# First batch's keys and values taken out of PSUM by two masked factors over all partitions, with three pieces of work re-ordered and the verdict's product later

## The chip, the cores and the metric

One core of one Trainium2 chip runs the whole kernel. The metric is the device time of one execution in microseconds; the runs' median counts.

## The reference

An attention with a memory of 32 slots (`M`) in 8 batches of 8 heads, followed by a layer of 8 experts with top-1 gating. Cut to what matters:

```python
# q, k, v: (8, 8, 576, 64); phi: (8, 8, 576, 32)
a = np.exp(phi - np.max(phi, axis=2, keepdims=True))
a = a / (np.sum(a, axis=2, keepdims=True) + 1e-09)
k_m = np.einsum('bhsm,bhsd->bhmd', a, k)          # keys of the memory
v_m = np.einsum('bhsm,bhsd->bhmd', a, v)          # values of the memory
scores = (1 / np.sqrt(64)) * np.matmul(q, k_m.transpose(0, 1, 3, 2))
attn = softmax(scores)                            # with 1e-09 in the sum
x = np.matmul(attn, v_m)                          # -> (4608, 512)
logits = x @ w_gate + modality_bias[modality_id]
e_idx = np.argmax(logits, axis=1); gate_w = softmax(logits)[e_idx]
out[mask_e] = gate_w * (np.maximum(x @ w1[e], 0) @ w2[e])   # mask_e: tokens of expert e
```

## The kernel before, in words

The kernel guesses one expert for all tokens from the first token's bias (`guess`), loads that expert's weights, and computes with them. At the end a verdict tells whether every token did choose that expert (`others`, `verdict`: DVE reduces `badp` to `bad`, PE adds it over the partitions by one product with `ones_c`, DVE writes `bad_i`, and every engine reads `bad_i` and branches). For other inputs a general path follows, which isn't entered here.

The 8 heads lie as 4 heads (`HG`) in each of 2 groups (`NG`); a group's 4 heads times 32 slots fill the 128 partitions. For a later batch the products of the memory (`kv_products`) are made head by head, each into its own 32 partitions and 64 columns. For the first batch, `first_products(t)` (t = 0 keys, t = 1 values) takes two heads at once: the weights of heads j and j+1 against both heads' 64 columns, so that 64 partitions x 128 columns are written, of which two blocks of 32 x 64 are wanted: head j even in columns 0 to 63, head j odd in columns 64 to 127. The other two blocks are products of one head's weights with the other head's keys. `first_sums` makes the sums of the weights into column 128.

`first_divide` adds EPS to the sums, takes the reciprocal `rec`, and `first_blocks(0, g)` copies the wanted blocks, times `rec`, into `keys`, head by head: 4 ACT instructions for group 0 and 4 DVE instructions for group 1. `first_blocks(1, g)` does the same for `values`, with 8 ACT instructions. `keys` are written twice side by side (the `o` axis of length 2).

What follows in the first batch: `first_keys` transposes the keys on PE and ACT copies them out (`kT`); `scores` multiplies them with the queries, which DVE has turned in place before (`q_turn`, in halves of heads); `soften` (DVE: turn, maximum, difference; ACT: exponential, one for each group in this part of the batch); `first_values` turns the values (`vT`); `value_products` multiplies vT with the first weights w1 (`raw`), giving `vwh` and `vwl` (an upper and a lower part of fp32); `normalise`, `a_split` (`xah`, `xal`); then `hidden` (x with vw, 128 or 320 columns wide) and `outputs` (with w2), which fill nearly all of the PE's time. `warm(n)` issues n products of zeros, fillers, into a bank that nobody reads.

The order of instructions is one program order for all engines, found when the kernel is built: `plan_first` and its like list stages by `add(name, kind, after, what, ...)`, and `weave` merges the attention's list with the experts' list by a model of durations (`TAKES`), floors (`floor`) and due times (`due`, in progress of the experts' products). Each engine runs its own instructions in that order, and waits by semaphores. Transfers are issued from SP's queue (and two small ones from ACT's).

Of the kernel before, what the change touches and what calls it, by code (L numbers as in the profile page):

```python
# [8 lines left out]
F32 = mybir.dt.float32  # L9
# [3 lines left out]
AF = mybir.ActivationFunctionType  # L13
# [41 lines left out]
def attn_moe(ctx: ExitStack, tc: tile.TileContext, q, k, v, phi, mod_id, w_gate, mod_bias, w1, w2, out):  # L55
# [22 lines left out]
    EPS = 1e-9  # L78
    BUSY = 92, 10

# [19 lines left out]
    ident = const.tile([P, P], F32, name="ident")  # L100
    ones_c = const.tile([P, 1], F32, name="ones_c")
    busy = const.tile([P, 512], BF16, name="busy")
    wg = const.tile([P, KCH, E], F32, name="wg")
# [235 lines left out]
    def first_products(t):  # L339

        pe = by_rows(live["pe", 0][0])
        pk = None if t else pair_of_banks(1)
        to = two_banks() if t else [pk[:, g] for g in range(NG)]
        live["first", t] = to

        tiles = [(j, g, slice(QP * g, QP * (g + 1))) for j in range(0, HG, 2) for g in range(NG)]
        for c in range(QC):
            for j, g, half in tiles:
                nc.tensor.matmul(  # L349
                    to[g][M * j:M * (j + 2), 0:2 * D].rearrange("p (j d) -> p j d", j=2),  # L350
                    lhsT=pe[half, c, j:j + 2].rearrange("p j m -> p (j m)"), rhs=kv_sb[half, t, j:j + 2, c * D:(c + 1) * D],
                    start=(c == 0), stop=(c == QC - 1), tile_position=(QP * g, M * j),
                )
# [11 lines left out]

    def first_divide():
        den = wk.tile([P, NG], F32, name="den")
        for g in range(NG):
            nc.vector.tensor_scalar_add(den[:, g:g + 1], live["first", 0][g][:, 2 * D:2 * D + 1], EPS)
        rec = wk.tile([P, NG, 1], F32, name="rec")  # L370
        nc.vector.reciprocal(rec[:, :, 0], den)
        live["rec"] = rec
        live["keys", 0] = wk.tile([P, 2, NG, 2, BL], F32, name="keys", bufs=2)
        live["values", 0] = wk.tile([P, NG, D], F32, name="values", bufs=2)
        for g in range(NG):
            first_blocks(0, g)

    def first_blocks(t, g):

        for j in range(HG):  # L380
            rows = slice(M * j, M * (j + 1))
            src = live["first", t][g][rows, D * (j % 2):D * (j % 2 + 1)]
            rec = live["rec"][rows, g]
            if t:
                nc.scalar.activation(live["values", 0][rows, g], src, AF.Copy, scale=rec)  # L385
                continue
            src = src.rearrange("p (u o d) -> p u o d", u=2, o=1).broadcast_to([M, 2, 2, BL])
            if g:
                nc.vector.tensor_scalar(live["keys", 0][rows, :, g], src, rec, None, op0=ALU.mult)
            else:  # L390
                nc.scalar.activation(live["keys", 0][rows, :, g], src, AF.Copy, scale=rec)

# [330 lines left out]
    def first_w2(c):  # L723
# [13 lines left out]
        "vwp": (1.15, ""), "vwu": (0.0, "A1.15"), "vwl": (0.0, "D1.35"),  # L737
# [42 lines left out]
    def plan_first():  # L780
# [4 lines left out]
        def nothing(n, name="pa"):  # L785
            add(("nothing", len(attention)), "nothing", [], warm, n, False, name)
# [13 lines left out]
        add(("exp", 0), "first exp", [("top", 0)], mem_exp, 0)  # L800
        nothing(4)
        add(("prepare",), "nothing", [], prepare)
        turns(0, 0, 11.0)
        add(("sums", 0), "first sums", [("exp", 0)], mem_sums, 0)
        add(("k", 0), "k0", [("exp", 0)], first_products, 0, floor=10.8)
        add(("ks", 0), "nothing", [("sums", 0)], first_sums)
        add(("kn", 0), "kn0", [("k", 0), ("sums", 0)], first_divide)
        turns(0, 1, 11.0)
        nothing(2)
        add(("kT", 0), "kT", [("kn", 0)], first_keys)  # L810
        add(("s", 0, 0), "s0", [("kT", 0), ("qt", 0, 0, 1)], scores, 0, 0, RA)
        add(("e", 0, 0, 0), "e", [("s", 0, 0)], soften, 0, 0, None, 0)
        add(("v", 0), "v0", [("exp", 0)], first_products, 1, floor=15.2)
        add(("vn", 0, 0), "vn0", [("v", 0)], first_blocks, 1, 0)
        add(("vn", 0, 1), "vn0", [("v", 0)], first_blocks, 1, 1)
        add(("e", 0, 0, 1), "e", [], soften, 0, 0, None, 1)
        add(("more", 0), "nothing", [], more_keys, 0)
        add(("kvT", 0), "vT", [("vn", 0, 1)], first_values)
        turns(1, 0, 16.8)
# [14 lines left out]
    def plan_steps(b, dues):  # L834
# [49 lines left out]
        if b == B - 1:  # L884
            stage(attention, ("v",), "verdict", [("others", pair)], verdict, due=due + 6.0)

# [125 lines left out]
    with tc.manual_schedule():  # L1012
# [148 lines left out]
```

## Time and profile before

| what | value |
|---|---|
| median of 3 runs | 407.84 us (406.47 to 408.52) |
| profiled execution | 408.26 us, its span 406.5 us |
| PE busy | 386.9 us, 95% of the span |
| DVE, ACT, POOL busy | 239.1, 146.5, 40.1 us |
| first hidden product | starts at 32.69 us |
| the verdict's product | starts at 360.79 us |

The span runs from the first instruction to the last of the profiled execution; its time has some 1.8 us around that. "PE" are the products, "PEld" the loads of their stationary operand, "SPq" SP's issue of transfers. In rows of instructions the columns are start, duration, engine, line, operation, out<-in, shapes, count, and in brackets the idle time of the engine before and who ended it. In rows of stretches the columns are the stretch, its length, the busy time and count of PE, PEld, DVE, ACT and POOL, the granted PE clock (1.00 is full), the DMA engines' busy share and GB/s. In rows of groups: busy us in total, mean ns of one, idle time before. In rows of waits: us in total, times, the longest. In rows of transfers: count, KB each, us from issue to landing.

### The profile page before, as it was taken

Reading aid. Unit: us, or ns where it says so; the run is one execution under the profiler, and the core shown is the slowest. Engines: PE = TensorE matmul, PEld = TensorE weight load, DVE = VectorE, ACT = ScalarE, POOL = GpSimd, SP = SyncE. Lnnn points to the kernel's source line nnn. Section 1 sums busy time; section 2 is a strip of 40 time slices with the busy share of each in tenths; the row PEclk is TensorE's granted clock in tenths of the full one; section 3 lists DMA queues with packets and bytes.
Section 4 is the critical chain, followed back from the end, with each engine's and each line's share of the span. In section 5 each row is a group of like instructions: output and inputs, shape, how many; then the busy total and the mean of one; then the engine's idle time right before and its main releaser. Section 6 shows DMA issues by size and latency. Waiting matters only on the chain.

```text
span 406.5 us, 10089 instructions
## 1 busy us (share of the span) xinstructions
PE 386.9 (95%) x4234; PEld 308.3 (76%) x4234; DVE 239.1 (59%) x586; ACT 146.5 (36%) x350; POOL 40.1 (10%) x79
## 2 busy tenths in 40 slices
PE   6579999999999999999999999999999999989994
PEld 2347796788778878787968879688877879678983
DVE  2556774976598546862587457764488437760400
ACT  1338243434433324342442325343342425341410
POOL 3136302002000200002000200002000200000000
PEclk8869999999999999999999999999999999999998
DMA  6998146915471391617611293523501011341112
GB/s 232 358 387 312 66 111 207 347 63 169 148 253 53 72 361 52 236 28 250 211 27 28 84 303 101 190 96 82 205 12 42 26 29 29 129 158 26 28 27 58
DMA packets 28967, 56.91 MB, mean 140 GB/s; under 512 B 3312, under 2 KB 8432, under 8 KB 28912
## 3 DMA queue, kind: packets, MB, share of 16 engines
q1 hardware_dynamic: 28624, 56.16, 41.6%
q8 instruction: 35, 0.57, 0.6%
q14 instruction: 20, 0.16, 0.1%
q10 hardware_dynamic: 288, 0.01, 0.0%
HBM read 37.29 MB, written 18.87 MB: 138 GB/s over the span
## 4 chain that ended last, share of the span: by engine, by line
PE 90%; DMA 3%; DVE 3%; ACT 2%; issue 1%; SPq 0%; ACTq 0%
PE pe L690 50%; PE pe L661 23%; PE pair L326 4%; PE pe L628 4%; PE pair L487 3%; DMA q_sb<-in_q_dram 3%; PE pair L575 1%; PE pe L349 1%; PE pair L141 1%; PE pair L628 1%; DVE hl L673 1%; ACT values L385 1%; PE pair L286 1%; ACT hh L670 0%; PE pair L464 0%
## 5 line engine op out<-in xcount | busy, mean ns | idle before, releaser
L690 PE MATMUL pe<-w2h,hh 128*128 128x512 f32 x288 | 117.7, 409 | 0.4 <-DVE hl L673 0.4
L690 PE MATMUL pe<-w2h,hl 128*128 128x512 f32 x288 | 112.6, 391 | 0.0
L690 PE MATMUL pe<-w2l,hh 128*128 128x512 f32 x288 | 110.4, 391 | 0.0
L673 DVE SCALAR_TENSOR_TENSOR hl<-pe,hh 128x256 fp32r<-128x256 f32 (+2 forms) x160 | 58.8, 393 | 55.0 <-ACT hh L670 54.3
L690 PEld LDWEIGHTS pe<-w2h,hh 128*128 128x128 f32 x288 | 54.0, 188 | 24.0 <-issue 11.5
L670 ACT ACTIVATE hh<-pe 128x256 fp32r<-128x256 f32 (+2 forms) x160 | 53.7, 361 | 38.9 <-PE pe L661 38.5
L690 PEld LDWEIGHTS pe<-w2l,hh 128*128 128x128 f32 x288 | 54.0, 188 | 12.0
L690 PEld LDWEIGHTS pe<-w2h,hl 128*128 128x128 f32 x288 | 54.2, 188 | 9.4
L703 ACT ACTIVATE ob<-pe,gates 128x512 f32<-128x512 f32 x36 | 24.7, 689 | 80.3 <-PE pe L690 39.5
L661 PE MATMUL pe<-xbh,vwh 128*128 128x320 f32 x128 | 39.9, 312 | 0.0
L661 PE MATMUL pe<-xbl,vwh 128*128 128x320 f32 x128 | 39.6, 309 | 0.0
L661 PE MATMUL pe<-xbh,vwl 128*128 128x320 f32 x128 | 39.5, 309 | 0.0
L661 PE MATMUL pe<-xah,vwh 128*128 128x256 f32 x128 | 36.2, 291 | 0.2 <-DVE hl L673 0.2
L661 PE MATMUL pe<-xal,vwh 128*128 128x256 f32 x128 | 35.1, 283 | 0.0
L661 PE MATMUL pe<-xah,vwl 128*128 128x256 f32 x128 | 35.0, 282 | 0.0
L257 POOL TENSOR_TENSOR t2sums<-exp 128x512 f32<-128x512 f32 x7 | 9.0, 1287 | 259.4 <-ACT exp L295 259.4
L514 DVE STREAM_TRANSPOSE a<-pair 128x256 f32<-128x256 f32 (+1 forms) x32 | 13.6, 460 | 24.6 <-PE pair L487 24.6
L661 PEld LDWEIGHTS pe<-xah,vwh 128*128 128x128 f32 x128 | 24.0, 191 | 1.7 <-DVE hl L673 1.0
L661 PEld LDWEIGHTS pe<-xbh,vwh 128*128 128x128 f32 x128 | 24.1, 188 | 0.6 <-issue 0.3
L661 PEld LDWEIGHTS pe<-xbl,vwh 128*128 128x128 f32 x128 | 24.1, 188 | 0.3
L661 PEld LDWEIGHTS pe<-xal,vwh 128*128 128x128 f32 x128 | 24.0, 191 | 0.3
L661 PEld LDWEIGHTS pe<-xbh,vwl 128*128 128x128 f32 x128 | 24.1, 188 | 0.0
(132 smaller groups left out, 441.1 us busy)
## 6 DMA issues: line engine op xcount, KB each, us to landing
kv_sb<-in_k_dram SPq DMA_DIRECT2D x8, 1152.0 KB, 5.9
kv_sb<-in_v_dram SPq DMA_DIRECT2D x8, 1152.0 KB, 9.6
out_dram<-ob SPq DMA_DIRECT2D x64, 128.0 KB, 2.4
q_sb<-in_q_dram SPq DMA_DIRECT2D x7, 1152.0 KB, 6.9
ph<-in_phi_dram SPq DMA_DIRECT2D x8, 576.0 KB, 4.1
raw<-in_moe_w_dram SPq DMA_DIRECT2D x2, 1024.0 KB, 8.9
raw<-in_moe_w_dram SPq DMA_DIRECT2D x1, 1280.0 KB, 11.3
out_dram<-ob SPq DMA_DIRECT2D x4, 256.0 KB, 2.0
```

The lines of the kernel that those rows point to most:

```text
L141: nc.tensor.transpose(dst, src, ident[:rows, :rows])
L257: eng.tensor_tensor(t2, src[:, :, 0:4 * M], src[:, :, 4 * M:8 * M], op=op)
L286: nc.tensor.matmul(pb[QP * g:QP * (g + 1), 0:P], lhsT=topc[:, g:g + 1].broadcast_to([P, QP]), rhs=ident, start=True, stop=True, tile_posit ...
L326: nc.tensor.matmul(live["kvp"][M * j:M * (j + 1), g], lhsT=pe[half, j, c * M:(c + 1) * M], rhs=kv_sb[half, :, j, c * D:(c + 1) * D], start ...
L487: nc.tensor.matmul(sc[g][M * j:M * (j + 1), a, c0 * BL:(c0 + n) * BL].rearrange("p (c t) -> p c t", t=BL), lhsT=kTs[b % 2][p0:p0 + BL, u, ...
L514: nc.vector.transpose(a[:, g].rearrange("p a c m -> p a (c m)"), sc[g][:, :, RA * part * BL:(RA * part + n) * BL])
L628: nc.tensor.matmul(pvs[g][M * j:M * (j + 1), :], lhsT=vT[b][rows, j, :], rhs=raw1[rows, j, cols], start=True, stop=True, tile_position=(D ...
L661: nc.tensor.matmul(ph[:, 0:n], lhsT=(vl if k == 2 else vh)[:, g, cols], rhs=xl if k == 1 else xh, start=(g == k == 0), stop=(g == NG - 1 a ...
L670: nc.scalar.activation(hs[0][:, f, h0:h0 + p1 - p0], ph[:, p0:p1], AF.Relu)
L673: nc.vector.scalar_tensor_tensor(hl, ph[:, p0:p1], 0.0, hh.bitcast(F32), op0=ALU.max, op1=ALU.subtract)
L690: nc.tensor.matmul(po, lhsT=tile_columns(hl if n == 1 else hh, f, t), rhs=(w2l if n == 2 else w2h)[:, f, :], start=(f == n == 0), stop=(f ...
L703: nc.scalar.activation(ob, po, AF.Copy, scale=gate_of(b, t))
```

## The change

A constant `places` of 128 x 2 holds, for each partition, 1 in column 0 where its head is even and 1 in column 1 where it is odd, else 0 (8 memsets of 32 x 1 on POOL at the start). `first_divide` multiplies the reciprocals with it: `recs` holds for each group the reciprocal for even heads (0 elsewhere) and for odd heads (0 elsewhere). `first_even(t)` takes columns 0 to 63 of all 128 partitions times the even factor, one ACT instruction for each group; `first_odd(t)` takes columns 64 to 127 times the odd factor and adds the even part, on DVE: four instructions for the keys (a group's two halves of 32 columns, each written twice), two for the values.

Beside it: the sums of the first batch are planned ahead of the first queries' turn; the second group's exponential ahead of the values' blocks; fillers are placed anew (86 small ones at the start instead of 92; 5 instead of 4 ahead of the key products, 4 new behind the sums' products, 2 behind the keys' turn instead of ahead of the division, 2 new ahead of the values' turn); and the verdict is due 12 instead of 6 after the last gate.

```diff
-    BUSY = 92, 10
+    BUSY = 86, 10
+    places = const.tile([P, 2], F32, name="places")
...
     def first_divide():
         den = wk.tile([P, NG], F32, name="den")
-        for g in range(NG):
-            nc.vector.tensor_scalar_add(den[:, g:g + 1], live["first", 0][g][:, 2 * D:2 * D + 1], EPS)
-        rec = wk.tile([P, NG, 1], F32, name="rec")
-        nc.vector.reciprocal(rec[:, :, 0], den)
-        live["rec"] = rec
+        nc.vector.tensor_scalar_add(den, live["sums0"], EPS)
+        rec = wk.tile([P, NG], F32, name="rec")
+        nc.vector.reciprocal(rec, den)
+        recs = wk.tile([P, 2, NG], F32, name="recs")
+        nc.vector.tensor_tensor(
+            recs, rec.rearrange("p (o g) -> p o g", o=1).broadcast_to([P, 2, NG]),
+            places.rearrange("p (e o) -> p e o", o=1).broadcast_to([P, 2, NG]), op=ALU.mult,
+        )
+        live["recs"] = recs
...
-        for g in range(NG):
-            first_blocks(0, g)
-
-    def first_blocks(t, g):
...
+        first_even(0)
+
+    def first_even(t):
+        live["even", t] = wk.tile([P, NG, D], F32, name=f"even{t}")
+        for g in range(NG):
+            nc.scalar.activation(
+                live["even", t][:, g], live["first", t][g][:, 0:D], AF.Copy, scale=live["recs"][:, 0, g:g + 1]
+            )
+
+    def first_odd(t):
+        def add(dst, src, even, g):
+            nc.vector.scalar_tensor_tensor(dst, src, live["recs"][:, 1, g:g + 1], even, op0=ALU.mult, op1=ALU.add)
+        for g in range(NG):
+            src, even = live["first", t][g][:, D:2 * D], live["even", t][:, g]
+            if t:
+                add(live["values", 0][:, g], src, even, g)
+                continue
+            for u in range(2):
+                half = slice(BL * u, BL * (u + 1))
+                add(live["keys", 0][:, u, g], *(
+                    x[:, half].rearrange("p (o d) -> p o d", o=1).broadcast_to([P, 2, BL]) for x in (src, even)
+                ), g)
...
         add(("exp", 0), "first exp", [("top", 0)], mem_exp, 0)
-        nothing(4)
+        nothing(5)
...
-        turns(0, 0, 11.0)
         add(("sums", 0), "first sums", [("exp", 0)], mem_sums, 0)
...
+        nothing(4)
         add(("kn", 0), "kn0", [("k", 0), ("sums", 0)], first_divide)
+        turns(0, 0, 11.0)
+        add(("ko", 0), "ko0", [("kn", 0)], first_odd, 0)
         turns(0, 1, 11.0)
+        add(("kT", 0), "kT", [("ko", 0)], first_keys)
         nothing(2)
-        add(("kT", 0), "kT", [("kn", 0)], first_keys)
...
         add(("v", 0), "v0", [("exp", 0)], first_products, 1, floor=15.2)
-        add(("vn", 0, 0), "vn0", [("v", 0)], first_blocks, 1, 0)
-        add(("vn", 0, 1), "vn0", [("v", 0)], first_blocks, 1, 1)
         add(("e", 0, 0, 1), "e", [], soften, 0, 0, None, 1)
+        add(("vn", 0), "vn0", [("v", 0)], first_even, 1)
+        add(("vo", 0), "ko0", [("vn", 0)], first_odd, 1)
...
-        add(("kvT", 0), "vT", [("vn", 0, 1)], first_values)
+        nothing(2, "pa")
+        add(("kvT", 0), "vT", [("vo", 0)], first_values)
...
-            stage(attention, ("v",), "verdict", [("others", pair)], verdict, due=due + 6.0)
+            stage(attention, ("v",), "verdict", [("others", pair)], verdict, due=due + 12.0)
...
+        for j in range(HG):
+            for e in range(2):
+                nc.gpsimd.memset(places[M * j:M * (j + 1), e:e + 1], float(j % 2 == e))
```

Three places of the resulting order. The first is DVE's queue from the sums (`t2top`, `sums`) to the queries' second turn; `q_sb` is a turn of the queries, `pair` is the PSUM pair with the key products. Before:

```order
L475 STREAM_TRANSPOSE q_sb_99<-q_sb_99 128x2x256
L305 TENSOR_TENSOR t2top<-exp 128x512
L306 TENSOR_TENSOR t2top<-t2top 128x256
L307 TENSOR_TENSOR sums<-t2top 128x128
L308 TENSOR_TENSOR sums<-sums,exp 128x128
L369 TENSOR_SCALAR den<-pair_361 128x1 x2
L371 RECIPROCAL rec<-den 128x2
L389 TENSOR_SCALAR keys<-pair_361,rec 32x2x64 x4
L475 STREAM_TRANSPOSE q_sb_99<-q_sb_99 128x2x256
```

and now, on the same engine at the same place:

```order
L307 TENSOR_TENSOR t2top<-exp 128x512
L308 TENSOR_TENSOR t2top<-t2top 128x256
L309 TENSOR_TENSOR sums<-t2top 128x128
L310 TENSOR_TENSOR sums<-sums,exp 128x128
L373 TENSOR_SCALAR den<-pair_364 128x2
L375 RECIPROCAL rec<-den 128x2
L377 TENSOR_TENSOR recs<-rec,places 128x4
L492 STREAM_TRANSPOSE q_sb_100<-q_sb_100 128x2x256
L397 SCALAR_TENSOR_TENSOR keys<-pair_364,recs,even_418 128x64 x4
L492 STREAM_TRANSPOSE q_sb_100<-q_sb_100 128x2x256
```

The first turn has moved from ahead of the sums to between the division and the key blocks. The second place is ACT's queue from the key blocks to the first weights' copy (`a` is an exponential of `soften`). Before:

```order
L391 ACTIVATE keys<-pair_361,rec 32x2x64 x4
L437 COPY kT_77<-pair_421 128x256
L522 ACTIVATE a<-a 128x256
L385 ACTIVATE values<-pe,rec 32x64 x8
L522 ACTIVATE a<-a 128x256
L445 COPY vT_79<-pe 128x128
L636 CAST vwh<-pair_532 128x512 x2
```

and now, on ACT:

```order
L390 ACTIVATE even_418<-pair_364,recs 128x64 x2
L454 COPY kT_78<-pair_427 128x256
L539 ACTIVATE a<-a 128x256 x2
L390 ACTIVATE even_516<-pe,recs 128x64 x2
L462 COPY vT_80<-pe 128x128
L653 CAST vwh<-pair_541 128x512 x2
```

The second exponential has moved from behind the value blocks to ahead of them. The third place is PE's queue around the verdict's product in the last batch, before:

```order
L661 MATMUL pe<-xal,vwh 128x256
L661 MATMUL pe<-xah,vwl 128x256
L616 MATMUL pair_4524<-ones_c,bad 1x1
L661 MATMUL pe<-xah,vwh 128x256
L661 MATMUL pe<-xal,vwh 128x256
```

and now, on PE:

```order
L707 MATMUL pe<-w2h,hh 128x512
L707 MATMUL pe<-w2h,hl 128x512
L707 MATMUL pe<-w2l,hh 128x512
L633 MATMUL pair_4615<-ones_c,bad 1x1
L707 MATMUL pe<-w2h,hh 128x512
L707 MATMUL pe<-w2h,hl 128x512
L707 MATMUL pe<-w2l,hh 128x512
```

It has moved from behind the first of eight groups of hidden products (6 each) to behind 18 of the output products that follow them. Elsewhere PE, DVE and ACT keep the order that they had, fillers aside.

More of the change, by code (lines that the diff above doesn't have):

```diff
@@ L344, in first_products @@
         live["first", t] = to
+        if t == 0:
+            live["sums0"] = pk[:, :, 2 * D]
         tiles = [(j, g, slice(QP * g, QP * (g + 1))) for j in range(0, HG, 2) for g in range(NG)]
@@ L375, in first_divide @@
         for g in range(NG):
-            first_blocks(0, g)
-    def first_blocks(t, g):
[L380 to L383, printed above, removed]
+            nc.scalar.activation(
[6 more added lines that the diff above has]
+            src, even = live["first", t][g][:, D:2 * D], live["even", t][:, g]
@@ L384, in first_blocks @@
             if t:
-                nc.scalar.activation(live["values", 0][rows, g], src, AF.Copy, scale=rec)
+                add(live["values", 0][:, g], src, even, g)
                 continue
[L387 to L391, printed above, removed]
+            for u in range(2):
[3 more added lines that the diff above has]
+                ), g)
```

2 rows, old and new, of the table TAKES are left out of this document.

## The prediction, made before the changed kernel was run

> **What bounds the kernel now.** I read the page's head and slices first, then the chain that ended last, the waits of PE, the granted clock in stretches of 3.4 us, and single rows for the durations.
>
> ```profile
> span 406.5 us, 10089 instructions
> ...
> PEclk8869999999999999999999999999999999999998
> ...
> 100.00:200.00 100.00, 99.84 (x1260) 80.69 (x1259) 64.13 (x160) 37.88 (x95) 8.12 (x12) 1.00 0.52 172
> ```
>
> After the start PE is busy without a gap (99.84 of 100 us in that stretch), at full clock from the fourth slice on. So a microsecond gained ahead of that stretch, or a PE wait taken out of it, comes off the end; an instruction saved on DVE or ACT inside it does not. The waits of PE say where such microseconds lie:
>
> ```profile
> PE pair L141 <- DVE keys L389: 3.1, 1, 3.1
> PE pe L141 <- ACT values L385: 2.6, 1, 2.6
> ```
>
> They are the first batch's blocks of keys and of values. A third wait of 1.15 us, for the verdict, has its row further down. All three are touched by the change. The chain shows the order of work between the two (start, duration, what):
>
> ```profile
> 13.11 0.59 DVE t2top L305
> ...
> 14.51 0.30 DVE sums L308
> ...
> 14.95 0.29 PE pair L360 x8
> ...
> 15.79 0.35 ACT keys L391
> ...
> 18.36 0.37 DVE keys L389
> ...
> 19.99 1.52 PE pair L487 x64
> 21.51 3.89 PE pe L349 x72
> 25.40 0.29 ACT values L385
> ...
> 27.94 0.42 ACT a L522
> ...
> 28.70 1.96 PE pair L628 x16
> ```
>
> Eight key blocks go one after another (15.79 to 18.73, ACT then DVE), eight value blocks likewise on ACT (25.40 to 27.92), and the sums wait for the queries' turn. PE idles meanwhile, and its clock (the column after POOL's count) answers:
>
> ```profile
> 11.30:14.75 3.45, 2.39 (x73) 1.98 (x72) 2.24 (x5) 0.63 (x2) 0.00 (x0) 1.00 1.06 372
> 14.75:18.15 3.40, 0.83 (x10) 0.35 (x10) 1.27 (x7) 1.43 (x4) 0.13 (x1) 1.00 1.10 315
> 18.15:21.55 3.40, 2.22 (x70) 1.35 (x74) 1.30 (x4) 0.37 (x1) 3.12 (x15) 0.50 1.05 387
> 24.95:28.35 3.40, 0.70 (x13) 0.27 (x5) 0.27 (x1) 2.85 (x9) 0.00 (x0) 1.00 1.06 387
> ```
>
> A stretch with PE 24% busy (0.83 of 3.40) is followed by half clock, one with 69% (2.39 of 3.45) kept it full, and 65% (2.22) did not bring it back. The 72 value products, which come then, take 3.89 us where the 72 key products took 2.20 at full clock (next rows).
>
> **The change, part by part.** The rows for its costs:
>
> ```profile
> 10.67 1.26 ACT L295 ACTIVATE exp<-exp 128x640 f32<-128x640 f32 x2 [7.72 <-DVE exp L292]
> 11.49 2.20 PE L349 MATMUL pair<-kv_sb,exp 64*64 64x128 f32 x72
> L673 DVE SCALAR_TENSOR_TENSOR hl<-pe,hh 128x64 fp32r<-128x64 f32 x32 | 6.9, 214 | 0.0
> L673 DVE SCALAR_TENSOR_TENSOR hl<-pe,hh 128x256 fp32r<-128x256 f32 x8 | 3.2, 417 | 2.3 <-ACT hh L670 2.3
> L405 ACT ACTIVATE values<-pair,rec 128x64 f32<-128x64 f32 x14 | 3.6, 319 | 0.0
> L587 DVE TENSOR_TENSOR lg<-lgT,bias 64x8 f32<-64x8 f32 x8 | 1.3, 158 | 0.1
> 9.70 1.81 PE L160 MATMUL pair<-busy 128*128 128x512 bf16 x4
> ```
>
> Sums ahead of the turn: they may start when the exponentials end (11.93) instead of 13.11; their four steps took 1.70 us (13.11 to 14.81), so they are ready at 13.65. Then the key products bind: the fifth filler ahead of them costs at most 0.45 us (four took 1.81), which moves their start from 11.49 to about 11.85, and their end to 14.05. The sums' products then start at 14.05 instead of 14.95. Gained: 0.9 us.
>
> Divide: one sum with EPS instead of two, and one more instruction for `recs` (the 64x8 product of 0.16 is nearest). From the sums' products to ACT's first block passed 0.84 us (14.95 to 15.79); I take 0.9. ACT starts at 14.95.
>
> Key blocks: two ACT factors of the shape 128x64 (0.32 each, the values of later batches) end at 15.6. DVE's turn of the queries (0.71) lies beside them and ends then too. Four DVE instructions follow; the hl row with 128x64 has their very shape, PSUM source and second operand included: 4 x 0.214 and gaps, 0.97 us, done at 16.6 instead of 18.73. Bounds: 0.16 each (the small product) to 0.42 (128x256), so 0.2 us better to 0.8 worse.
>
> From the last key block to the scores passed 1.26 us (18.73 to 19.99). One transpose can now start before the last block (0.2 less), but two fillers wait for the kT copy and stand ahead of the scores: 0.45 us at full clock, 0.9 at half. Scores start at 18.1, or 18.5 at half clock, instead of 19.99. The second queries' turn (0.71 after 16.6) is done at 17.3 and hidden. For the scores I keep 1.5 us at either clock, so the value products run 19.6 to 21.8 at full clock, 20.0 to 23.9 at half.
>
> Second exponential ahead of the values: DVE's two softening steps took 2.6 us (in the next rows 21.52 to 24.08, where the queries' turn follows), so ACT (0.42, the chain at 27.94) ends it at 22.75 (full) or 23.15 (half). At full clock it now stands in the values' way for 0.95 us; at half it is hidden behind the products. Two factors (0.64) and the last DVE step (0.25) give 23.65 or 24.85 for the values instead of 27.92. Transpose, copy and issue took 0.78: the first weights' products start at 24.4 or 25.65 instead of 28.70.
>
> What is late next: on DVE a turn of the queries, the sums of a and the normalising are queued behind the two value instructions.
>
> ```profile
> 21.52 0.45 DVE L514 STREAM_TRANSPOSE a<-pair 128x256 f32<-128x256 f32 x1 [2.05 <-PE pair L487]
> ...
> 24.08 0.83 DVE L475 STREAM_TRANSPOSE q_sb<-q_sb 128x640 f32<-128x640 f32 x1
> ...
> 28.39 0.42 DVE L530 TENSOR_REDUCE sa<-a 128x8 f32<-128x256 f32 x1 [3.17 <-ACT a L522]
> ...
> 30.07 0.77 DVE L546 STREAM_TRANSPOSE aT<-a 128x256 f32<-128x256 f32 x2
> 31.72 0.63 ACT L555 CAST xah<-aT 128x512 fp32r<-128x512 f32 x1
> 32.69 1.30 PE L661 MATMUL pe<-xah,vwh 128*128 128x256 f32 x8
> ```
>
> From the turn to aT's end these need 3.65 us (0.8 for the turn, 0.4 for one sum, 2.45 from 28.39 to 30.84 for the rest), then 0.65 for xah. At full clock the first hidden product starts at 23.65 + 3.65 + 0.65 + 0.05 = 28.0, instead of 32.69: 4.7 us gained. At half clock DVE gives 29.2, PE (25.65 and most of the 3.99 us from 28.70 to 32.69) about 29.4: 3.3 us gained.
>
> Costs at nothing: the eight memsets on POOL, since `places` is first read at 14.8 and DVE's first work waits for the phi transfer, not for POOL; were POOL made late by them, only the expert's guess and its weights' transfers would move, and those have 1.9 us to spare (rival T). Six small fillers fewer move only idle time. No transfer is moved in a queue. From the hidden products on, PE's rows stand as before but for the verdict.
>
> The verdict's product moves 12 us of plan later. Before, PE stood still in the midst of hidden products:
>
> ```profile
> 359.36 0.28 PE L661 MATMUL pe<-xah,vwl 128*128 128x256 f32 x1
> 360.79 0.19 PE L616 MATMUL pair<-ones_c,bad 128*1 128x1 f32 x2 [1.15 <-DVE bad L614]
> 360.90 0.38 PE L661 MATMUL pe<-xah,vwh 128*128 128x256 f32 x1
> ...
> 266.27 0.28 PE L661 MATMUL pe<-xah,vwl 128*128 128x256 f32 x1
> 266.39 0.28 PE L661 MATMUL pe<-xah,vwh 128*128 128x256 f32 x1
> ```
>
> At the same place two batches earlier, the next group follows after 0.12 us; here after 1.54. The product itself keeps its 0.11, so 1.3 us go (between the wait's 1.15 and 1.42). In its new place it follows 18 output products (some 4 us after the last hidden one), when DVE has long reduced `bad`; its result would be there near 369, and the end is past 400.
>
> The sum: 4.7 + 1.3 = 6.0 us. The profiled execution took 408.26 us (1.8 around its span of 406.5), 0.42 above the median of 407.84. The before's three runs differ by 2.05 us, so I don't take the 0.42 off as well: 408.26 - 6.0 = **402.3 us**.
>
> The clock decides between 4.7 and 3.3. In 14.75 to 18.15, PE's work is then a rest of the four fillers, the two transposes, two fillers and the first scores, about 1.7 of 3.4 us or 50%, between the 24% that lost the clock and the 69% that kept it, with no pause over 1.5 us, where the waits around the drops were 3.1 and 2.6. It is nearer to the kept one by its pauses, so I take full clock. [...]
>
> **Rivals.**
> C, half clock as before: the fillers don't hold it. For it, the stretch 18.15 to 21.55, 65% busy, did not raise it. 408.26 - 3.3 - 1.3 = 403.7.
> L, half clock reaches further: the 3.4 us stretches fall elsewhere, so that as well as C one stretch of dense products runs at half clock, 1.7 us more: 405.4. Against it, the weights' products come first and keep PE busy from 25.65 on, so that the clock should be up by 29.
> V, PE's stop at the verdict was also one for a free bank, and remains: 403.6. Against it, 266.39.
> T, transfers are the floor: the DMA engines are full (share 1.05 and more) in every stretch shown above.
>
> ```profile
> 12.65 2.71 SPq L202 DMA_DIRECT2D raw<-in_moe_w_dram  x2
> ...
> raw<-in_moe_w_dram SPq DMA_DIRECT2D x2, 1024.0 KB, 8.9
> raw<-in_moe_w_dram SPq DMA_DIRECT2D x1, 1280.0 KB, 11.3
> ```
>
> If the first weights set the pace, only the verdict's 1.3 is left: 407.0, no difference to tell. Against it: the two halves of w1, issued from 12.65, land by these rows some 8.9 us on, near 21 and 23.5, and the first part of w2, issued next at 15.5, near 27; I need them at 24.4, 25.5 and 28.9.
> S, slower: the clock stays half in the dense hidden and output products. Each 3.4 us cost 1.7, so it outweighs the 6.0 and 0.5% more only from 16 us of half clock after 28 us on; at 20 us the time is 412. The PEclk line shows 9 in every slice after the third.
>
> **How the numbers follow.** My forecast 0.45, C 0.27, L 0.13, V 0.05, T 0.07, S 0.03. About 0.5% (2 us) is what a measurement of this kernel can tell from no change. Faster: the first four, 0.90; same: T, 0.07; slower: S, 0.03. The range runs from 402.3 less the 0.42 and half the runs' spread (400.9) to just short of L (405.2).
>
> **What would show it.** Right: DVE's key blocks end near 16.6, scores start near 18, value products take 2.2 us, hidden products start near 28, granted clock 1.00 from 11 us on, no PE wait for `bad`. C: value products 3.9 us, hidden near 29.4. Wrong altogether: hidden products after 31, or a wait of PE on raw.

## The result, and the profile after

The changed kernel takes 402.31 us in the median of four runs (401.36 to 403.41), beside 408.00 for the kernel before on the same chip: a ratio of 0.9868, with an interval from 0.9826 to 0.9909. The profiled execution took 401.36 us, 6.9 less than that of before. The head of its page:

```profile
span 399.6 us, 10090 instructions
...
PEclk9999999999999999999999999999999999999999
```

The clock's line has 9 from the first slice on, where before it began 8869. The waits of PE (total in us, times, longest):

```profile
PE pe L143 <- DVE values L397: 1.2, 1, 1.2
PE pair L143 <- DVE keys L397: 1.1, 1, 1.1
```

The two waits for the first batch's blocks are still there, but 1.1 and 1.2 us long instead of 3.1 and 2.6. The wait for `bad` has no row any more. The verdict's product now stands at 362.89 in the timeline, among output products that follow each other without a gap:

```profile
362.57 0.39 PE L707 MATMUL pe<-w2l,hh 128*128 128x512 f32 x1
362.89 0.19 PE L633 MATMUL pair<-ones_c,bad 128*1 128x1 f32 x2
363.00 0.50 PE L707 MATMUL pe<-w2h,hh 128*128 128x512 f32 x1
```

The start, in the timeline (start, duration, engine, line, what; in brackets the engine's idle time before and what ended it), by the instructions whose times the prediction gave:

```profile
13.98 0.26 PE L364 MATMUL pair<-ones_c,sums 64*64 64x1 f32 x8
14.98 0.52 ACT L390 ACTIVATE even<-pair,recs 128x64 f32<-128x64 f32 x2 [3.01 <-DVE recs L377]
15.53 0.86 DVE L397 SCALAR_TENSOR_TENSOR keys<-pair,recs,even 128x64 f32<-128x64 f32 x4
17.88 1.07 PE L504 MATMUL pair<-q_sb,kT 32*32 32x128 f32 x64
18.88 2.19 PE L353 MATMUL pe<-kv_sb,exp 64*64 64x128 f32 x72
21.64 0.42 ACT L539 ACTIVATE a<-a 128x256 f32<-128x256 f32 x1 [0.87 <-DVE a L537]
22.29 0.49 DVE L397 SCALAR_TENSOR_TENSOR values<-pe,recs,even 128x64 f32<-128x64 f32 x2 [0.69 <-ACT even L390]
23.51 1.66 PE L645 MATMUL pair<-raw,vT 64*32 64x512 f32 x16 [0.35 <-ACT vT L462]
26.32 0.62 ACT L572 CAST xah<-aT 128x512 fp32r<-128x512 f32 x1
26.99 1.21 PE L678 MATMUL pe<-xah,vwh 128*128 128x256 f32 x8
```

The first hidden product starts at 26.99 instead of 32.69, 5.7 us sooner. What follows it keeps its length, and that is the measure for all the experiments below. From the first hidden product to the end of the span pass 399.6 - 26.99 = 372.6 us; before, 406.5 - 32.69 = 373.8. The same two numbers of every profile taken here:

| profile | span | first hidden product | rest | wait for `bad` |
|---|---|---|---|---|
| before | 406.5 | 32.69 | 373.8 | yes |
| verdict back (e1) | 401.4 | 27.72 | 373.7 | yes |
| before with fillers (e7) | 405.3 | 31.84 | 373.5 | yes |
| after | 399.6 | 26.99 | 372.6 | no |
| after again (e0) | 400.0 | 27.59 | 372.4 | no |
| verdict only (e2) | 405.0 | 32.71 | 372.3 | no |
| no fillers (e3) | 400.9 | 28.11 | 372.8 | no |
| old blocks (e4) | 403.3 | 30.47 | 372.8 | no |
| turn first (e5) | 399.6 | 27.10 | 372.5 | no |
| even first (e6) | 401.5 | 29.05 | 372.5 | no |
| one turn (e9) | 398.8 | 26.57 | 372.2 | no |
| one turn, 70 (e10) | 397.7 | 25.16 | 372.5 | no |
| small 92 (e11) | 399.8 | 27.61 | 372.2 | no |
| small 70 (e12) | 399.6 | 27.01 | 372.6 | no |

Without the wait for `bad` the rest is 372.2 to 372.8 us (mean 372.49 of eleven), with it 373.5 to 373.8 (mean 373.65 of three). So the verdict is worth 1.16 us, and whatever moves the first hidden product moves the end by as much: 5.70 + 1.16 = 6.86, the 6.9 us between the two spans.

### The profile page after: what moved, and what is told of

Read it like the earlier page. It is cut to its first block, busy times and chain, and to the rows that moved or that the text cites. A ratio compares the mean times of both kernels' runs of the same rounds, so it can differ in the third digit from the quotient of the medians.

```text
span 399.6 us, 10090 instructions
## 1 busy us (share of the span) xinstructions
PE 385.6 (96%) x4235; PEld 306.5 (77%) x4235; DVE 239.1 (60%) x588; ACT 143.6 (36%) x342; POOL 40.7 (10%) x87
## 4 chain that ended last, share of the span: by engine, by line
PE 90%; DVE 5%; DMA 1%; ACT 1%; issue 1%; ACTq 0%
PE pe L707 52%; PE pe L678 23%; PE pair L328 4%; PE pe L645 4%; PE pair L504 3%; DMA ph<-in_phi_dram 1%; PE pair L592 1%; PE pair L143 1%; PE pair L162 1%; PE pair L288 1%; DVE vwl L658 1%; PE pair L353 1%; DVE hl L690 1%; DVE t2top L259 0%; DVE q_sb L492 0%
## 5 line engine op out<-in xcount | busy, mean ns | idle before, releaser
L707 PEld LDWEIGHTS pe<-w2h,hh 128*128 128x128 f32 x288 | 54.0, 188 | 23.9 <-issue 11.5
L707 PEld LDWEIGHTS pe<-w2l,hh 128*128 128x128 f32 x288 | 54.0, 188 | 12.1
L678 PEld LDWEIGHTS pe<-xah,vwh 128*128 128x128 f32 x128 | 23.9, 191 | 1.9 <-DVE hl L690 1.0
```

Of the source, the lines that this page charges most:

```text
L678: nc.tensor.matmul(ph[:, 0:n], lhsT=(vl if k == 2 else vh)[:, g, cols], rhs=xl if k == 1 else xh, start=(g == k == 0), stop=(g == NG - 1 a ...
L707: nc.tensor.matmul(po, lhsT=tile_columns(hl if n == 1 else hh, f, t), rhs=(w2l if n == 2 else w2h)[:, f, :], start=(f == n == 0), stop=(f ...
```

## The experiments

All were timed in five rounds against the kernel before on the same chip. "After" means the changed kernel.

**The changed kernel once more (e0).** No edit.

> The changed kernel once more, as the measure for the others of this call. Expected 402.3 us, in two groups some 1.7 us apart (401.4 and 403.2 in the four runs so far), by whether one stretch of 3.4 us at half clock more falls into the start.

401.66 us, ratio 0.9861 (0.9844 to 0.9877). Its profile shows the other case of the clock, though the program is the same. Stretches of 3.4 us, laid on the steps of the clock (PE's busy time first; the clock follows POOL's count), of this run and then of the first profile of after:

```profile
14.88:18.28 3.40, 1.77 (x39) 0.63 (x37) 2.21 (x7) 0.89 (x3) 0.20 (x2) 1.00 1.10 325
18.28:21.67 3.39, 3.39 (x112) 2.97 (x83) 2.24 (x6) 0.42 (x1) 3.11 (x14) 0.50 1.05 387
```

```profile
15.30:18.71 3.41, 1.85 (x68) 1.09 (x68) 1.68 (x6) 0.57 (x2) 0.58 (x4) 1.00 1.07 338
18.71:22.12 3.41, 2.90 (x97) 2.07 (x74) 2.51 (x6) 0.90 (x3) 3.10 (x13) 1.00 1.06 387
```

The second pair is laid on the step up of that profile, at 11.88. PE is busy 1.77 of 3.40 us in the one and 1.85 of 3.41 in the other; the clock was lost in the one and kept in the other. What it costs is seen in the timeline of e0:

```profile
19.22 3.37 PE L353 MATMUL pe<-kv_sb,exp 64*64 64x128 f32 x72
24.22 1.17 PE L645 MATMUL pair<-raw,vT 64*32 64x512 f32 x16 [0.35 <-ACT vT L462]
27.59 1.22 PE L678 MATMUL pe<-xah,vwh 128*128 128x256 f32 x8 [0.32 <-ACT xah L572]
```

The value products take 3.37 us instead of 2.19, but hidden products start only 0.6 us later than with the clock kept, because the second exponential, which stands in the values' way at full clock, is then hidden behind the products.

**The verdict back in its old place (e1).**

```diff
-            stage(attention, ("v",), "verdict", [("others", pair)], verdict, due=due + 12.0)
+            stage(attention, ("v",), "verdict", [("others", pair)], verdict, due=due + 6.0)
```

> The changed kernel with the verdict due 6 instead of 12 after the last gate, so that its product stands again behind the first group of hidden products of the last batch. Theory (PE waits there for DVE's bad and loses 1.3 us that nothing gives back): 1.3 us slower than the changed kernel, with a PE wait of 1.1 us for bad. Rival (the stop was for a free bank, or is made up for later): no difference, below 0.4 us.

403.87 us, ratio 0.9909 (0.9894 to 0.9925). The wait is back, in its timeline:

```profile
354.31 0.28 PE L678 MATMUL pe<-xah,vwl 128*128 128x256 f32 x1
355.74 0.19 PE L633 MATMUL pair<-ones_c,bad 128*1 128x1 f32 x2 [1.15 <-DVE bad L631]
```

The ratio lies 0.0048 above that of e0, about 2.0 us with 0.9 to either side; the 1.16 us of the table lie within that. The profile lost the clock as that of e0 did (value products of 3.51 us, hidden products at 27.72).

**The verdict alone (e2).** The kernel before, with its `due + 6.0` made `due + 12.0` and nothing else.

> The kernel before with only the verdict's product moved (due 12 instead of 6 after the last gate). Theory (a PE wait that nothing gives back): 1.3 us faster than before, ratio 0.9968. Rival (made up for later, or another wait in its place): no difference.

406.57 us, ratio 0.9978 (0.9967 to 0.9990), 0.9 us faster (0.4 to 1.35). PE waits for `bad` no more, and the first hidden product starts at 32.71, where it did: in the profiles the two parts of the change add up. In the medians they do so only just: the start alone (e1 against before) is worth 3.7 us and the verdict alone 0.9, together 4.6, where e0 has 5.7; the difference of 1.1 us is about as large as its uncertainty (1.0).

**The old blocks in the new order (e4).** The head-by-head blocks of before, with the new order, fillers and verdict.

```diff
+    def first_blocks(t):
+        for g in range(NG):
+            for j in range(HG):
...
-        add(("ko", 0), "ko0", [("kn", 0)], first_odd, 0)
+        add(("ko", 0), "ko0", [("kn", 0)], first_blocks, 0)
...
-        add(("vn", 0), "vn0", [("v", 0)], first_even, 1)
-        add(("vo", 0), "ko0", [("vn", 0)], first_odd, 1)
+        add(("vn", 0), "vn0", [("v", 0)], first_blocks, 1)
```

> The changed kernel with the blocks taken out head by head as before (4 ACT and 4 DVE instructions for the keys, 8 ACT for the values, no masked factors), all else as changed: sums first, exponential first, fillers, verdict. Theory (the masked factors make the way from the reciprocals to the scores 1.4 us shorter and from the value products to the values' turn 1.7 us): hidden products at 30 to 31 us instead of 27.0, so 3 to 4 us slower than the changed kernel, near 405.5 to 406. Rival (the fillers and the order do it, by the clock): within 1.5 us of the changed kernel.

405.69 us, ratio 0.9957 (0.9936 to 0.9977), 3.9 us slower than e0 by the ratios. Its waits of PE:

```profile
PE pair L143 <- DVE keys L391: 2.7, 1, 2.7
PE pe L143 <- ACT values L387: 2.1, 1, 2.1
```

They are near the 3.1 and 2.6 of before, and hidden products start at 30.47. This profile lost the clock from 19.61 to 23.02 (0.50 granted from 20.20 to 23.00), so of the two profiles of after, that of e0, which lost it too, is the nearer to compare with. So 2.9 to 3.5 of the 5.7 us at the start belong to the masked factors (30.47 against 26.99 and 27.59), and 2.2 (from 32.69) come with the order and the fillers alone.

**No fillers (e3).** After, without nine big fillers in the first batch: the seven that the change added and the two that stood ahead of the scores already.

```diff
-        nothing(5)
+        nothing(4)
         add(("prepare",), "nothing", [], prepare)
...
-        nothing(4)
         add(("kn", 0), "kn0", [("k", 0), ("sums", 0)], first_divide)
...
-        nothing(2)
         add(("s", 0, 0), "s0", [("kT", 0), ("qt", 0, 0, 1)], scores, 0, 0, RA)
...
-        nothing(2, "pa")
         add(("kvT", 0), "vT", [("vo", 0)], first_values)
```

> The changed kernel without its nine added fillers (4 ahead of the key products, none behind the sums' products, none between the kT copy and the scores, none ahead of the values' turn). Theory (the shorter blocks alone leave pauses too short for the clock to drop): not slower, up to 0.7 us faster, since the key products start 0.45 us sooner and the scores 0.6 us, value products still 2.2 us. Rival (the fillers hold the clock): the clock falls to half at the scores, value products 3.9 us, 1 to 2 us slower than the changed kernel.

401.88 us, ratio 0.9867 (0.9849 to 0.9886): no difference from e0. Its profile has both effects. The scores start sooner (17.54 instead of 17.88), since no filler stands ahead of them, and run at half clock, as do all the value products:

```profile
17.54 1.52 PE L504 MATMUL pair<-q_sb,kT 32*32 32x128 f32 x64 [0.46 <-ACT kT L454]
18.99 4.12 PE L353 MATMUL pe<-kv_sb,exp 64*64 64x128 f32 x72
28.11 1.21 PE L678 MATMUL pe<-xah,vwh 128*128 128x256 f32 x8 [0.40 <-ACT xah L572]
```

PE was busy 1.28 of the 3.40 us ahead of the drop (13.32 to 16.72). This execution is 0.85 us above the median of its kernel; in the medians the fillers cost about what they save.

**The kernel before with fillers in its pauses (e7).** Before, with twelve more fillers ahead of the keys' transposes and ten ahead of the values' transpose; blocks, order and verdict as they were.

```diff
-        nothing(2)
+        nothing(14)
         add(("kT", 0), "kT", [("kn", 0)], first_keys)
...
         add(("more", 0), "nothing", [], more_keys, 0)
+        nothing(10, "pa")
```

> The kernel before with 12 more fillers (14 instead of 2) behind the sums' products and 10 ahead of the values' turn, nothing else changed. They lie in PE's pauses of 3.1 and 2.6 us. Theory (the clock is a part of the gain by itself): value products 2.2 instead of 3.9 us, weights' products 1.1 to 1.4 instead of 2.0, scores' start as before, so 2 to 2.5 us faster than before, near 405.7. Rival (what counts is only the order and number of the blocks' instructions): no gain over 0.5 us, since DVE's softening (2.6 us) and ACT's blocks follow the scores in any case.

407.07 us, ratio 0.9982 (0.9970 to 0.9994): 0.7 us, far less than expected. The value products run at full speed, but the blocks that follow take what they took:

```profile
20.79 2.20 PE L349 MATMUL pe<-kv_sb,exp 64*64 64x128 f32 x72
23.03 2.54 ACT L385 ACTIVATE values<-pe,rec 32x64 f32<-32x64 f32 x8 [0.32 <-PE pe L349]
25.99 1.57 PE L160 MATMUL pair<-busy 128*128 128x512 bf16 x6 [2.04 <-issue]
27.35 0.42 PE L141 MATMUL pe<-ident,values 128*128 128x128 f32 x1
31.84 1.30 PE L661 MATMUL pe<-xah,vwh 128*128 128x256 f32 x8
```

The values' transpose comes at 27.35, and hidden products only 0.85 us sooner than before. A filler also stood still for 2.04 us in the midst of its group, with no releaser that the profile shows ("issue"); the last section comes back to it. That stop left PE busy for 1.37 of 3.41 us (23.79 to 27.20), the clock fell to half behind it (0.52 granted from 27.10 to 30.50), and the first sixteen of the weights' products took 1.96 us, as in before. So this run does not show what a clock kept to the end would be worth with the old blocks.

**The queries' turn first again (e5).** After, with `turns(0, 0, 11.0)` back ahead of the sums.

```diff
+        turns(0, 0, 11.0)
         add(("sums", 0), "first sums", [("exp", 0)], mem_sums, 0)
...
         add(("kn", 0), "kn0", [("k", 0), ("sums", 0)], first_divide)
-        turns(0, 0, 11.0)
```

> The changed kernel with the first turn of the queries back ahead of the sums. Theory (the key products end near 14.05 and hide the sums only as long as those are done by then; with the turn ahead they are done near 14.8): the keys' way starts 0.7 us later, but the turn no longer stands between the division and the key blocks, where it ended with ACT's even factors and cost nothing; 0.6 to 0.8 us slower than the changed kernel. Rival (the queue of DVE after the scores absorbs it): no difference.

402.62 us, ratio 0.9883 (0.9863 to 0.9903), not told apart from after. DVE's queue in its profile, and in that of before, says why:

```profile
11.19 0.70 DVE L492 STREAM_TRANSPOSE q_sb<-q_sb 128x512 f32<-128x512 f32 x1
12.00 0.69 DVE L307 TENSOR_TENSOR t2top<-exp 128x512 f32<-128x512 f32 x1
```

```profile
12.40 0.71 DVE L475 STREAM_TRANSPOSE q_sb<-q_sb 128x512 f32<-128x512 f32 x1 [1.17 <-DMA q_sb<-in_q_dram]
13.04 0.65 DVE L305 TENSOR_TENSOR t2top<-exp 128x512 f32<-128x512 f32 x1
```

Before, the turn waited for the queries until 12.40. Here they had landed by 11.19, and the turn fits into the pause while ACT computes the exponentials; the sums start at 12.00 either way. So the edit didn't undo what it was to undo, because the queries came sooner, though their transfer is issued at 1.78 us in both. With the turn waiting as in before the sums would be late by about a microsecond. What brought the queries sooner shows in the traces: the number of small fillers at the start. From issue to landing the first queries take, in e11 below (after with 92 small fillers and no other edit) and then here with 86:

```profile
q_sb<-in_q_dram SPq DMA_DIRECT2D x1, 512.0 KB, 10.6
q_sb<-in_q_dram SPq DMA_DIRECT2D x1, 512.0 KB, 9.2
```

All four profiles with 92 (before, e2, e7, e11) have 10.6 or 10.7 us, and the other ten, with 86 or 70, 9.1 to 9.3 (10.2 in e6, where the first loads landed late). By which way the fillers act on the transfer stays open.

**The even factors ahead of the second softening (e6).** After, with `first_even` for the values ahead of `soften`, so that the second exponential no longer stands in the values' way.

```diff
-        add(("e", 0, 0, 1), "e", [], soften, 0, 0, None, 1)
         add(("vn", 0), "vn0", [("v", 0)], first_even, 1)
+        add(("e", 0, 0, 1), "e", [], soften, 0, 0, None, 1)
```

> The changed kernel with the values' even factors planned ahead of the second softening, so that on ACT they stand ahead of the second exponential; DVE's odd factors stay behind the softening. Theory (at full clock the value products are over at 21.1 us and the exponential, which waits for DVE until 21.6, holds the even factors up): values out at 22.1 instead of 22.8, hidden products 0.65 us sooner, 0.65 us faster than the changed kernel. Rival (the reordering was a gain, since the exponential delays what follows it on DVE): 0.2 to 0.5 us slower.

402.52 us, ratio 0.9863 (0.9849 to 0.9878): no gain. Its profile was late from the start: phi, which DVE's first work waits for, landed a microsecond later (that work starts at 7.38 instead of 6.38), and the key products then began at half clock (0.50 granted from 11.30 to 14.75; they took 3.02 us instead of 2.19), so that the first factor of the keys starts at 16.92 instead of 14.98. From that factor to the first hidden product pass 12.1 us, where after has 12.0. The values' way is shorter as planned (from the first value product to the values' end 3.21 us instead of 3.90), but the first weights' products stand still ahead of the last two of sixteen, the cast of `vwh` waits for them on ACT until 27.41, and the cast of `xah` stands behind it there (28.37):

```profile
24.77 1.09 PE L645 MATMUL pair<-raw,vT 64*32 64x512 f32 x14 [0.35 <-ACT vT L462]
26.33 1.04 PE L645 MATMUL pair<-raw,vT 64*32 64x512 f32 x2 [0.47 <-issue]
```

**One turn earlier as well (e9).** e6, and the third turn of the queries moved from behind the values to ahead of the first softening, so that it no longer delays the normalising.

```diff
+        turns(1, 0, 16.0)
         add(("e", 0, 0, 0), "e", [("s", 0, 0)], soften, 0, 0, None, 0)
...
-        turns(1, 0, 16.8)
```

> The changed kernel with the values' even factors ahead of the second softening, and the third turn of the queries (heads 0 and 1 of the second part) planned ahead of the first softening, where DVE waits for the scores (17.0 to 18.9 us), instead of behind the values. Theory (DVE's queue from the odd factors to aT sets the first hidden product): 0.65 us from the factors and 0.75 us from the turn, hidden products at 25.6 us, 1.4 us faster than the changed kernel, near 400.9. Rival (the turn waits for its queries, which land near 17.5, and holds the softening up; or the weights' products or w2's transfer become the bound): gain of 0.7 us or less.

401.87 us, ratio 0.9866 (0.9848 to 0.9884): no gain in the median, and only 0.4 us at the first hidden product (0.3 of which the profile already had at the first factor of the keys, 14.66). The first weights' products start at 22.41, 1.1 us sooner than in after, and stop in the same place:

```profile
22.41 1.09 PE L645 MATMUL pair<-raw,vT 64*32 64x512 f32 x14 [0.35 <-ACT vT L462]
23.85 1.04 PE L645 MATMUL pair<-raw,vT 64*32 64x512 f32 x2 [0.36 <-issue]
26.57 1.22 PE L678 MATMUL pe<-xah,vwh 128*128 128x256 f32 x8
```

**The same with 70 small fillers at the start (e10).** e9 with `BUSY = 70, 10` instead of `86, 10`. It takes 16 tiny products and their weight loads off PE's program ahead of everything else; later products of the program keep their order.

> The kernel with the even factors ahead of the second softening and the third queries' turn ahead of the first softening, now with 70 instead of 86 small fillers at the start, which moves every later PE instruction 32 places forward against the blocks in which PE's instructions are fetched. Theory (the last two of the first 16 weights' products waited to 23.85 us for a block of instructions, whose transfer of 16 KB started at 21.2 to 21.5 behind a full DMA): no such pause, the first 16 products take 1.1 instead of 2.5 us, hidden products at 25.3 instead of 26.6 us, 1.2 us faster than with 86, near 400.6. Rival (the pause is for w1's transfer or for a bank): the pause stays at the same products and nothing is gained.

401.42 us, ratio 0.9849 (0.9826 to 0.9873), its lowest run 399.52. The pause is gone, and the first hidden product comes at 25.16:

```profile
22.32 1.09 PE L645 MATMUL pair<-raw,vT 64*32 64x512 f32 x16 [0.35 <-ACT vT L462]
25.16 1.24 PE L678 MATMUL pe<-xah,vwh 128*128 128x256 f32 x8
26.85 1.14 ACT L737 CAST w2h<-raw 128x512 fp32r<-128x512 f32 x2 [0.77 <-DMA raw<-in_moe_w_dram]
```

The loads now begin to be felt: at 23.66 the second half of these products has waited 0.23 us for `raw`, and ACT waits 0.77 us for the first part of w2, which lands near 26.85. The rest of the span is still 372.5, so the second wait does not reach the end yet. This is the fastest version tried, 1.8 us sooner than after at the first hidden product and 1.9 in the span (0.4 of them already at the first factor of the keys, 14.58), but in the medians only 0.9 us, and the intervals overlap: that it beats after is not shown.

**The number of small fillers alone (e12 with 70, e11 with 92).** After with `BUSY = 70, 10`, and with `92, 10` as before.

> The changed kernel with 70 small fillers at the start instead of 86 (PE's instructions 32 places forward against the fetched blocks). Theory: the pause of 0.6 us in the first weights' products goes; these take 1.1 us instead of 1.7; since DVE's queue (aT, then xah) sets the first hidden product within 0.1 us of PE here, the gain is 0 to 0.3 us. Rival (another cause): the pause stays.

> The changed kernel with 92 small fillers at the start as before the change, so that PE's instructions come 12 places later against the fetched blocks. Theory (a block of instructions arrives near 24.1 us): the pause within the first 16 weights' products comes some 12 instructions (6 products) earlier and lasts up to 1 us instead of 0.6, 0.2 to 0.5 us slower than the changed kernel. Rival (the pause has another cause): it stays ahead of the last two products, no difference.

With 70: 402.59 us, ratio 0.9873 (0.9852 to 0.9894). With 92: 402.62 us, 0.9869 (0.9847 to 0.9891). With 70 the pause is gone, and nothing is gained by it, since the cast of `xah` sets the first hidden product:

```profile
23.64 1.09 PE L645 MATMUL pair<-raw,vT 64*32 64x512 f32 x16 [0.35 <-ACT vT L462]
27.01 1.21 PE L678 MATMUL pe<-xah,vwh 128*128 128x256 f32 x8 [0.40 <-ACT xah L572]
```

With 92 the profiled execution lost the clock as e0 did (value products of 3.44 us), so that the weights' products began only at 24.24, later than the pause of after ended (24.13), and there is no pause to be seen: inconclusive for the question that it was run for.

## Why the prediction was right

By its own steps, with the profile of after:

- *Sums*: said, their products at 14.05 instead of 14.95, ACT's first factor at 14.95. Measured: 13.98 and 14.98. The reason given, that the turn ahead of the sums holds them up, holds where the queries come as late as in before: in e11 they do, and with the turn moved the first factor starts at 15.02. But "six small fillers fewer move only idle time" was wrong: they bring the queries some 1.4 us sooner, so that in e5 the turn was ahead of the sums and held up nothing, and the first factor started at 15.19, against 15.79 in before. Either edit gives most of this gain, and the prediction credits it to one.
- *Key blocks*: said, two factors of 0.32 and four DVE steps, done at 16.6. Measured: 0.52 for both factors and 0.86 for the four, done at 16.39. The DVE price, taken from the `hl` row of the same shape, held for the four together (0.97 was said); ACT's group mean of 0.319 was too high as the step from one to the next: in after the two factors have a mean of 0.310, but the second starts before the first has ended.
- *Scores*: said, at 18.1 and 1.5 us long "at either clock". Measured: 17.88, and value products 1.00 us later at full clock, 1.45 in e3 at half. This is the term that was mis-sized at the start: 0.5 us.
- *Value products*: said, 2.2 us at full clock, from 19.6 to 21.8. Measured: 2.19, from 18.88 to 21.07.
- *Second exponential*: said, in the values' way for 0.95 us. Measured: its end at 22.06, 0.99 after the last value product. In e6 this wait is gone and nothing is gained: PE's pause among the weights' products and, behind it on ACT, the cast of `xah` then set the hidden products.
- *Values, hidden products*: said, 23.65 and 28.0. Measured: 22.78 and 26.99. Between the two lie 4.21 us, where 4.35 were said, and they end, as said, with DVE's normalising and the cast of `xah`.
- *Verdict*: said 1.3; measured 1.16 by the table, 0.9 (0.4 to 1.35) alone.

So the gain was 5.7 + 1.16 = 6.9 us in the profiled executions, where 6.0 was predicted. That the median met 402.3 is in part luck: the gain was under-estimated by 0.9 us, and the median lies 0.95 us above the profiled execution.

The rivals. **C**, half clock as before, is not a rival to the forecast but a mixture with it: of six profiles of the new order with its big fillers in place (after, e0, e1, e5, e11, e12) three kept the clock and three lost it. The prediction chose full clock at an estimated 1.7 us of work in 3.4; measured are 1.85 in after, which kept it, and 1.77 in e0, which lost it, so the choice was right for the first profile by luck. What was wrong there is its price. The prediction charged 1.4 us (hidden products at 28.0 or 29.4); measured are 26.99 to 27.10 with the clock, and 27.59 to 27.72 without, 0.5 to 0.7. Two of its steps failed. Half clock lasted one stretch of 3.4 us (18.28 to 21.67 in e0), so that the value products ended 1.5 us later than with the clock kept (22.59 against 21.07), where 2.1 were charged. And the weights' products ran at full clock again (1.17 us), so that PE's path, charged with most of the 3.99 us of before, did not bind. **L** and **S**, half clock in dense products, don't show in the clock of after (1.00 granted from 11.88 to 396). **V**, the stop at the verdict for a free bank, fell with the row at 362.89 and with e2, where the stop is gone and the rest of the span is 372.3. **T**, the transfers as the floor, is false for this change: no wait on `raw` stands ahead of the hidden products in after, and even in e10, 1.8 us sooner, the waits for `raw` are 0.23 and 0.77 us and the rest of the span keeps its length. It is not far off, though.

What stays open: the runs of one kernel lie up to 4.1 us apart (404.42 to 408.54 for e4), and in after and e0 they gather at two values some 1.6 us apart. Of each kernel only one execution was profiled here, and the clock's 0.5 to 0.7 us explain less than half of it. The mean granted clock of every execution does not settle it: in after 0.993 and 0.995 stand beside the two shorter times and 0.988 and 0.990 beside the two longer, but in e11 0.999 stands beside 402.68 us and 0.988 beside 401.68.

## What to carry to other kernels

Find the first instruction behind which the kernel runs without a gap, and note in each profile when it starts: the rest of the span (372.2 to 372.8 us in eleven profiles here) varied by 0.6 us where the runs of one kernel varied by up to 4.1, and priced the start and the verdict apart more sharply than the medians could (1.16 us for the verdict, where e2 gives 0.4 to 1.35). Masking a whole tile with two per-partition factors, in place of one instruction per block, is worth it where the blocks stand on the path (six steps, 1.41 us, for eight, 2.94). Work that is added to keep PE's clock up must be charged as delay: in the medians of e0 and e3 (401.66 and 401.88 us) it cost as much as it saved.

## What the runs showed that was not expected

**PE pauses with no cause named, most likely for its own instructions.** Pauses marked "issue" in the midst of a group stand in the profiles of after (0.44 us in the first row of weight loads below; the products take 1.66 us instead of 1.09), e5 (0.31), e6 (1.38), e7 (2.04) and e9 (1.26, the second row).

```profile
24.13 0.13 PEld L645 LDWEIGHTS pair<-raw,vT 64*32 64x32 f32 x2 [0.44 <-issue]
```

```profile
23.85 0.13 PEld L645 LDWEIGHTS pair<-raw,vT 64*32 64x32 f32 x2 [1.26 <-issue]
```

The view of the DMA queues has a queue of the kind "instruction" (q8; in the whole of after 35 transfers with 0.57 MB, 16 KB each). In each of these profiles it shows one transfer some 2.5 us ahead of the end of the pause, while the loads keep the engines full (q1 at 100.3% in e9, 104.6% in e7). Of after, from 21.4 to 22.0 us (packets, MB, share):

```profile
q1 hardware_dynamic: 110, 0.22, 100.4%
q8 instruction: 1, 0.02, 10.9%
```

| profile | the transfer shows in | the pause ends |
|---|---|---|
| after | 21.5 to 21.8 | 24.13 |
| e5 | 21.5 to 21.8 | 24.20 |
| e9 | 21.2 to 21.5 | 23.85 |
| e6 | 23.6 to 23.9 | 26.33 |
| e7 | 23.5 to 23.8 | 25.99 |

In e10 the transfer shows at the same time as in e9 (21.2 to 21.5), but with 16 small fillers fewer PE does not stop at 23.85. That the place in PE's program decides is shown by this pair and by after and e12, one execution of each; that the transfer carries PE's instructions is inferred. Two things beside its time speak for it. In e0, e1 and e11 it shows at 21.5 to 21.8 as in after, and PE, which comes to these products only at 24.22 or later, does not pause. And the transfer ahead of it in the same queue shows at 7.1 us with 92 small fillers (before), at 12.6 with 86 (after) and in 15.2 to 15.5 with 70 (e12), so in these three its time moves with the number of PE's small fillers. If the inference holds, these waits cost from 0.31 us (e5) to 2.04 us (e7), where the DMA engines are full and PE comes early.

**The clock at half load is not settled by the busy share.** In stretches laid on each profile's own steps of the clock, 1.28 busy of 3.40 us lost it (e3), 1.77 lost it (e0) and 1.85 kept it (after), but 1.69 of 3.41 kept it as well (e4, 23.02 to 26.43). At half clock 2.22 did not bring it back in before and 2.77 did in e7 (10.14 to 13.55). In e3 the same busy time brought it back once and once did not:

```profile
9.93:13.34 3.41, 2.96 (x47) 2.24 (x48) 2.58 (x6) 1.26 (x2) 0.00 (x0) 0.50 1.06 385
13.34:16.75 3.41, 1.29 (x46) 1.24 (x40) 2.17 (x10) 0.52 (x2) 0.00 (x0) 1.00 1.12 313
16.75:20.17 3.42, 2.96 (x90) 2.17 (x93) 1.50 (x4) 0.37 (x1) 1.99 (x11) 0.50 1.05 382
20.17:23.58 3.41, 2.94 (x56) 2.54 (x48) 1.54 (x5) 1.25 (x4) 3.02 (x10) 0.50 1.05 383
```

The least busy of these stretches still had 1.28 us of work, and no threshold on the share alone fits these rows. What else decides stays open.

**Sixty-four small products feel the clock too**: the scores take 1.07 us at full clock (after) and 1.52 at half (e3), where the prediction had kept them at 1.5.
